# Attention outputs turned by VectorE in 32-squares and divided by their row sums after the gather

## The chip, the core and the metric

The kernel runs on one core of a Trainium2 chip. The core has five engines with queues of their own: TensorE (PE in the profile, with its weight loads as PEld), VectorE (DVE), ScalarE (ACT), GpSimd (POOL) and SyncE (SP), which here only issues DMAs. An instruction starts when those ahead of it in its engine's queue have started and the semaphores that it waits for are set. Sixteen DMA engines move data between DRAM and SBUF, and within SBUF. The metric is the time of one execution on the device, in microseconds (us); of several runs the median is given.

## The reference

The first half is attention with a threshold, for 8 batches, 8 heads, 576 positions and 64 dimensions per head. The second half routes each of the 4608 tokens to one of 8 experts by a hash of its id, and runs a two-layer network.

```python
scores = scale * np.matmul(q, k.transpose(0, 1, 3, 2))
thresh = np.max(scores, axis=-1, keepdims=True) - tau
scores = np.where(scores >= thresh, scores, -1000000000.0)
scores = scores - np.max(scores, axis=-1, keepdims=True)
attn = np.exp(scores)
attn = attn / (np.sum(attn, axis=-1, keepdims=True) + 1e-09)
attn_out = np.matmul(attn, v)
x = attn_out.transpose(0, 2, 1, 3).reshape(B * S, H * D)   # 4608 x 512
expert_idx = token_ids * 2654435761 % E                    # E = 8, F = 1024
for e in range(E):
    xe = x[expert_idx == e]
    out[expert_idx == e] = np.maximum(xe @ w1[e], 0.0) @ w2[e]
```

## The kernel before

**Attention** goes by pairs: two heads of one batch, 32 pairs `p` in all (8 batches for each of 4 head pairs `hp`). A pair has five steps `s`, and one loop counts them through, `n = 5 p + s`. Step 0 takes the last 64 queries of both heads, steps 1 to 4 take 128 queries each. The order of all instructions is written out by hand in that loop (it stands under `manual_schedule`, so no scheduler moves them), and it is a software pipeline. In step `n`:

- `score(n + 1, j)` (L219): PE multiplies queries by keys into one of two PSUM tiles `sc`.
- `negate(n, j)` (L230): VectorE copies the negated scores to `ns` and keeps the row's minimum. GpSimd then makes the threshold `thr` from it (L237). `expo(n, j)` (L244): ScalarE's exponential.
- `mask(n - 1, j)` (L255): VectorE compares with `thr`, multiplies with the exponential into `w`, and sums each row into `rs`.
- `turn_w(n - 2, j)` (L266): PE turns `w`, in 64-wide pieces, through the one PSUM tile `tr`; ScalarE copies the result to `wT` (L282, L287).
- `av_part` (L297): PE multiplies `wT` by the values of pair `q = p - 1` into the PSUM tile `av`, which then holds outputs as 128 dimensions (two heads) by positions. ScalarE copies that to `oT` (`put_oT`, L313), the first 320 columns in step 2, the last 256 in step 4.

So a pair's outputs are complete when the next pair is in its step 4. In step 0 of the pair after that (`s == 0 and p >= 2`), `turn_o` turns them back with ten PE instructions (L266 again, but into `av` from `oT`), and `put_xm` (L336) multiplies them on VectorE by the reciprocals `rec` of the row sums, to which `add_eps` (L327) added 1e-9 on GpSimd and L670 took the reciprocal. Three DMAs on SP's queue then write the normalized rows of the pair to the scratch tensor `x_dram` in DRAM, `x_scratch` in the profile: 512 pieces of 512 bytes (L342) and twice 64 of 256 bytes (L347).

SP's queue also has the loads, in order of the loop: keys and queries of pair `p + 2` and values of `p + 1` in step 0 (L174 to L196), then the x writes, then in some pairs a 2 MB weight tensor in step 2 (pairs 20, 22, 24, 26). GpSimd scales the next pair's keys in step 1 (`scale_k`, L199).

**Routing** runs beside attention. `route()` has small VectorE operations, one or two per step, in pairs 0 to about 16; `scatters()` writes each token's number to its expert's slots with GpSimd DMAs after that.

**The first expert begins early.** From pair 26 on (`n >= G0`), the steps 2, 3 and 4 each issue one `fetch_0` on GpSimd: an indirect DMA (L110) that gathers 128 tokens' rows for one head pair into `xg`, for five blocks of tokens and the first three head pairs, 15 in all. `x_dram` is tracked as a whole: a gather waits for the x writes issued before it, and an x write waits for the gathers issued before it. After the last pair the fourth head pair follows (five gathers). `early_xT` turns `xg` on PE (L555): the first three head pairs at `n == LAST` (160, one past the last step), the fourth after the last gathers. `early_h` (L579) has 48 pieces of the first expert's first product, and `fill(n)` puts `n` of them into PE's queue at places where PE would have nothing to do.

**Experts.** For expert `e`, `turn_x(e + 1)` turns the next expert's gathered rows in 32-squares on VectorE (L856), and 16 DMAs put the squares in place (L861); `gemm1` (L784) and `gemm2` (L802, L815) are PE's products, with evictions on ScalarE and VectorE; the output rows leave by indirect DMAs (L841). `fetch(e + 2)` gathers while expert `e` is in its second product.

## Time and profile before

| | us |
|---|---|
| median of 3 runs | 1004.77 |
| lowest, highest | 1003.88, 1005.04 |
| the profiled execution | 1003.3 |
| its span, first to last instruction | 1001.3 |
| PE busy in the span | 983.8 |
| VectorE busy | 517.7 |
| ScalarE busy | 436.9 |
| GpSimd busy | 291.7 |
| DMA packets | 145779, 117.07 MB |
| of these under 512 bytes | 59860 |

How to read it: the profile comes from one execution, recorded by the hardware. A line of a timeline has the start in us from the beginning of the span, the length in us, the engine, the line of the kernel, the operation, what it writes `<-` what it reads, its shape, and in brackets the idle time before it with what ended it. A group line has the busy time and the mean in ns of one instruction. Lengths of successive instructions of one engine overlap by some hundredths, so the spacing of starts is what one more instruction costs. The end of a matmul is modelled, and a PE that shows as busy need not be at its peak. A wait for several semaphores is put down to the one that came last by the profile; where the engine named had long been done, it was another, often a DMA.

### The profile page before, as it was taken

Reading aid. Unit: us, or ns where it says so; the run is one execution under the profiler, and the core shown is the slowest. Engines: PE = TensorE matmul, PEld = TensorE weight load, DVE = VectorE, ACT = ScalarE, POOL = GpSimd, SP = SyncE. Lnnn points to the kernel's source line nnn. Section 1 sums busy time; section 2 is a strip of 40 time slices with the busy share of each in tenths; the row PEclk is TensorE's granted clock in tenths of the full one; section 3 lists DMA queues with packets and bytes.
Section 4 is the critical chain, followed back from the end, with each engine's and each line's share of the span. In section 5 each row is a group of like instructions: output and inputs, shape, how many; then the busy total and the mean of one; then the engine's idle time right before and its main releaser. Section 6 shows DMA issues by size and latency. Waiting matters only on the chain.

```text
span 1001.3 us, 20487 instructions
## 1 busy us (share of the span) xinstructions
PE 983.8 (98%) x7562; PEld 653.9 (65%) x7562; DVE 517.7 (52%) x1378; ACT 436.9 (44%) x714; POOL 291.7 (29%) x413
## 2 busy tenths in 40 slices
PE   7999999999999999999999999999999999999995
PEld 4666666666666666666766857768578577685773
DVE  7999999999999999994311010010101100200000
ACT  5988888888988889883200000010010000100000
POOL 3233323377676335550321030030210300300101
PEclk9999999999999999999999999999999999999998
DMA  7355544564467677410166344272352533801001
GB/s 182 74 129 141 129 117 112 136 141 107 92 185 169 154 195 194 114 49 25 39 189 185 116 105 143 91 211 89 106 163 84 158 91 104 222 1 39 27 10 57
DMA packets 145779, 117.07 MB, mean 117 GB/s; under 512 B 59860, under 2 KB 120280, under 8 KB 145680
## 3 DMA queue, kind: packets, MB, share of 16 engines
q1 hardware_dynamic: 135408, 96.41, 37.9%
q0 software_dynamic: 7824, 18.91, 6.1%
q8 instruction: 61, 1.00, 0.4%
q10 hardware_dynamic: 2448, 0.44, 0.2%
q14 instruction: 38, 0.31, 0.1%
HBM read 81.99 MB, written 22.37 MB: 104 GB/s over the span
## 4 chain that ended last, share of the span: by engine, by line
PE 87%; issue 6%; SPq 2%; DMA 2%; ACT 1%; DVE 1%; POOL 0%; POOLq 0%; ACTq 0%
PE sc L784 20%; PE av L297 17%; PE sc L219 15%; PE o_ps L802 12%; PE tr L266 10%; PE sc L815 8%; PE sc L579 3%; SPq L835 2%; PE av L266 1%; DMA out_dram<-o_last,gidx 1%; DMA out_dram<-o,gidx 1%; ACT w L244 1%; PE xT_ps L596 0%; PE sc L596 0%; ACT wT_a L287 0%
## 5 line engine op out<-in xcount | busy, mean ns | idle before, releaser
L244 ACT ACTIVATE w<-ns,nmx 128x576 f32<-128x576 f32 x288 | 220.3, 776 | 33.2 <-DVE ns L230 33.1
L784 PE MATMUL sc<-xT,w_sb 128*128 128x304 f32 x896 | 230.4, 419 | 0.0
L255 DVE SCALAR_TENSOR_TENSOR w<-ns,thr,w 128x576 f32<-128x576 f32 x288 | 225.4, 814 | 0.4 <-POOL thr L237 0.4
L784 PEld LDWEIGHTS sc<-xT,w_sb 128*128 128x128 f32 x896 | 170.2, 190 | 61.4 <-issue 3.3
L230 DVE TENSOR_SCALAR_CACHE_REDUCE ns<-sc 128x576 f32<-128x576 f32 x288 | 205.2, 744 | 6.3 <-PE sc L219 5.6
L219 PE MATMUL sc<-k_sb,q 64*128 64x288 f32 (+1 forms) x1280 | 179.2, 426 | 0.6 <-DVE ns L230 0.4
L802 PE MATMUL o_ps<-w_sb,h 128*128 128x512 f32 (+2 forms) x400 | 166.2, 575 | 0.0
L266 PEld LDWEIGHTS tr<-ident,w 64*128 64x128 f32 x2624 | 106.6, 139 | 88.7 <-ACT wT_b L287 26.3
L237 POOL TENSOR_SCALAR thr<-nmx,drop 128x2 f32<-128x2 f32 (+1 forms) x160 | 101.8, 637 | 176.7 <-DVE ns L230 163.4
L792 DVE TENSOR_SCALAR h<-sc 128x608 f32<-128x608 f32 x28 | 22.2, 791 | 240.9 <-PE sc L784 240.9
L266 PE MATMUL tr<-ident,w 64*128 64x64 f32 x2624 | 139.3, 231 | 2.7 <-ACT wT_a L287 2.0
L804 ACT COPY o<-o_ps 128x512 f32<-128x512 f32 (+2 forms) x25 | 14.2, 569 | 274.5 <-PE o_ps L802 248.1
L802 PEld LDWEIGHTS o_ps<-w_sb,h 128*128 128x128 f32 x400 | 74.9, 190 | 86.8 <-issue 84.7
L841 POOL DMA_INDIRECT out_dram<-o,gidx x24 | 23.9, 996 | 324.0 <-ACT o L804 291.4
L219 PEld LDWEIGHTS sc<-k_sb,q 64*128 64x128 f32 (+1 forms) x1280 | 93.0, 179 | 22.9 <-DVE ns L230 9.7
L297 PE MATMUL av<-wT_a,v 128*64 128x320 f32 (+1 forms) x704 | 100.4, 418 | 0.0
L790 ACT ACTIVATE h<-sc 128x608 f32<-128x608 f32 x28 | 19.0, 677 | 182.0 <-PE sc L784 182.0
L815 PE MATMUL sc<-h,w_sb 128*128 128x224 f32 x512 | 98.2, 352 | 0.0
L815 PEld LDWEIGHTS sc<-h,w_sb 128*128 128x128 f32 x512 | 96.9, 190 | 1.1
L287 ACT COPY wT_a<-tr 128x512 f32<-128x512 f32 (+1 forms) x128 | 81.7, 638 | 20.7 <-PE tr L266 20.1
L287 ACT COPY wT_b<-tr 128x512 f32<-128x512 f32 (+1 forms) x128 | 81.2, 634 | 6.4 <-PE tr L266 4.0
L297 PE MATMUL av<-wT_b,v 128*64 128x256 f32 x640 | 83.2, 389 | 0.0
(118 smaller groups left out, 547.9 us busy)
## 6 DMA issues: line engine op xcount, KB each, us to landing
w_sb<-in_moe_w_dram SPq DMA_DIRECT2D x16, 2048.0 KB
q<-in_q_dram SPq DMA_DIRECT2D x62, 288.0 KB
v<-in_v_dram SPq DMA_DIRECT2D x32, 256.0 KB
x_scratch<-xm SPq DMA_DIRECT2D x32, 256.0 KB
xT<-xq SPq DMA_DIRECT2D x84, 80.0 KB
k_sb<-in_k_dram SPq DMA_DIRECT2D x31, 144.0 KB
k_sb<-in_k_dram SPq DMA_DIRECT2D x32, 112.0 KB
o_last<-oq SPq DMA_DIRECT2D x210, 16.0 KB
```

Of the source, the lines that this page charges most:

```text
L219: nc.tensor.matmul(sc[out_rows, i, 0:S2], lhsT=q_sb[rows, h, q0:q1], rhs=k_sb[rows, h], start=True, stop=True)
L230: nc.vector.tensor_scalar(out=ns[:].rearrange("p (i s) -> p i s", i=2), in0=sc[:, :, 0:S2], scalar1=-1.0, scalar2=None, op0=ALU.mult, op1= ...
L237: nc.gpsimd.tensor_scalar(out=thr[:, 0:j + 1], in0=stats[n][0][:, 0:j + 1], scalar1=drop[:], scalar2=None, op0=ALU.add)
L244: nc.scalar.activation(w, nss[n, j][:], AF.Exp, bias=stats[n][0][:, j:j + 1], scale=-1.0)
L255: nc.vector.scalar_tensor_tensor(out=w, in0=nss.pop((n, j))[:], scalar=stats[n][1][:, j:j + 1], in1=w, op0=ALU.is_le, op1=ALU.mult, accum_ ...
L266: nc.tensor.transpose(dst[:, r, 64 * c:64 * c + 64], src[rows, c0:c0 + P], ident[rows, rows])
L287: nc.scalar.copy(dst, tr[:, :, 0:64 * n_c].rearrange("p r (c q) -> p r c q", c=n_c))
L297: nc.tensor.matmul(av[64 * j:64 * j + 64, g, c0:c1], lhsT=v_sb[:, c, 64 * j:64 * j + 64], rhs=wT[g][:, i, c0:c1], start=(c == 0), stop=stop)
L579: nc.tensor.matmul(h_ps[:, i, 0:CH], lhsT=w1_sb[:, co, fo * P:fo * P + P], rhs=xT_0[:, co, i * CH:i * CH + CH], start=(co == 0), stop=(co ...
L784: nc.tensor.matmul(h_ps[:, i, 0:width], lhsT=w1_sb[:, co, fo * P:fo * P + P], rhs=xT[:, co, i * width:i * width + width], start=(co == 0), ...
L802: nc.tensor.matmul(o_ps[:, 0:width], lhsT=h_sb[:, fo, FIRST[kt]:FIRST[kt] + P], rhs=w2_sb[:, fo, cols], start=(fo == 0), stop=(fo == FO - 1))
L815: nc.tensor.matmul(oT_ps[:, i, c * OW:c * OW + OW], lhsT=w2_sb[:, fo, co * P:co * P + P], rhs=h_sb[:, fo, FIRST[KF]:CAP], start=(fo == ord ...
```

## The change

Attention's outputs are no longer turned by PE, nor normalized before they are written. `oT` becomes two tiles, of 320 and 256 columns. `turn_o(p, g)` is now one VectorE transpose in 32 by 32 squares from `oT[g]` into `xo`; the first stands in step 3 between the two `negate`s of the step, the second in step 0 where `put_xm` stood. In `xo` a partition holds one position out of 32 and a run of 32 dimensions, so `put_x` writes pieces of 128 bytes: four DMAs of 576 pieces each. `put_sums`, in step 1, writes the raw row sums to two further columns beside each head pair's 128 (three DMAs of 8- and 4-byte pieces); a row of `x_dram` grows from 512 to 520 numbers, and gathers bring the sums along. The steps take the 64 odd queries first instead of last, so that the 32-squares fit.

The division comes after the gather. For the first expert's first three head pairs GpSimd adds 1e-9 per gathered block (step 1 of pairs 27 to 31), VectorE takes one reciprocal, and GpSimd multiplies: two blocks in step 3 of pair 31 and three in step 4. For the fourth head pair VectorE does all three, between the last gathers and `early_xT`; `fill` is redistributed round it (22 pieces before, 8 after, and the two ahead of the former last `turn_o` are dropped). For the other experts `normalized` does it on VectorE in `turn_x`. At the start the identity is made inside the hand-written order, PE gets 17 instead of 16 turns of it, and the keys' scale is computed in one operation ahead of `drop`.

```diff
+    DX = P + 2
+    x_dram = nc.dram_tensor("x_scratch", (N, HP * DX), FP32, kind="Internal").ap()
...
+    xr_0 = [consts.tile([P, KT, n, 2], FP32, name=f"xr_{n}") for n in (HP - 1, 1)]
...
+    def normalize(engine, dst, xg, rec):
+        engine.tensor_tensor(
+            out=dst.rearrange("p h (j d) -> p h j d", j=2),
+            in0=xg[:, :, 0:P].rearrange("p h (j d) -> p h j d", j=2),
+            in1=rec[:, :, :, None].to_broadcast([P, rec.shape[1], 2, D]), op=ALU.mult)
...
-        def turn_o():
-            turn(av, oT, [(P * (t + 1), P * (t + 1)) for t in range(NQ)] + [(64, 0)])
+        def turn_o(p, g):
+            if g == 0:
+                xo = a_x.tile([P, S // 32, 32], FP32, name="xo")
+                xos[p] = xo
+            c0, c1 = ((0, WA // 32), (WA // 32, S // 32))[g]
+            nc.vector.transpose(out=xos[p][:, c0:c1],
+                                in_=oT[g][:].rearrange("p (c s) -> p c s", s=32))
...
+        def put_x(p):
+            r0, c0 = x_place(p)
+            xo = xos.pop(p)
+            for i in range(4):
+                nc.sync.dma_start(
+                    out=x_dram[r0:r0 + S, c0 + 32 * i:c0 + 32 * i + 32].rearrange(
+                        "(c s) m -> s c m", s=32),
+                    in_=xo[32 * i:32 * i + 32])
+
+        def put_sums(p):
+            r0, c0 = x_place(p)
             rs = rss.pop(p)
-            for i, cols in ((0, 9), (9, 1)):
-                nc.gpsimd.tensor_scalar(out=rec[:, i:i + cols], in0=rs[:, i - i // 9:i - i // 9 + cols],
-                                        scalar1=1e-9, scalar2=None, op0=ALU.add)
...
+                out=x_dram[r0 + 64:r0 + S, c0 + P:c0 + DX].rearrange("(t p) j -> p t j", p=P),
+                in_=rs[:, 0:8].rearrange("p (t j) -> p t j", j=2))
             for j in range(2):
+                nc.sync.dma_start(out=x_dram[r0:r0 + 64, c0 + P + j:c0 + P + j + 1],
+                                  in_=rs[64 * j:64 * j + 64, 8:9])
...
                 if s == 1 and 0 <= q < NP:
-                    add_eps(q)
+                    put_sums(q)
...
-                if s == 2 and 0 <= q < NP:
-                    nc.vector.reciprocal(recs[q][:], recs[q][:])
-                if n == LAST + NS:
-                    fill(2)
-                if s == 0 and p >= 2:
-                    turn_o()
...
+                if s == 3 and 0 <= q < NP:
+                    turn_o(q, 0)
                 if s == 0 and p >= 2 and n != LAST:
-                    put_xm(p - 2)
+                    turn_o(p - 2, 1)
+                    put_x(p - 2)
...
+                k = p - (NP - KT)
+                if s == 1 and 0 <= k < KT:
+                    nc.gpsimd.tensor_scalar(out=xr_0[0][:, k], in0=xg_bufs[k][:, 0:HP - 1, P:DX],
+                                            scalar1=1e-9, scalar2=None, op0=ALU.add)
+                if n == LAST - 3:
+                    nc.vector.reciprocal(xr_0[0][:], xr_0[0][:])
+                for k in {LAST - 2: (0, 1), LAST - 1: (2, 3, 4)}.get(n, ()):
+                    normalize(nc.gpsimd, xg_bufs[k][:, 0:HP - 1, 0:P], xg_bufs[k][:, 0:HP - 1],
+                              xr_0[0][:, k])
...
-            fill(FO * 2 * (CO - 1) - 18)
+            fill(FO * 2 * (CO - 1) - 26)
+            for kt in range(KT):
+                nc.vector.tensor_scalar(out=xr_0[1][:, kt], in0=xg_bufs[kt][:, HP - 1:HP, P:DX],
+                                        scalar1=1e-9, scalar2=None, op0=ALU.add)
+            nc.vector.reciprocal(xr_0[1][:], xr_0[1][:])
+            for kt in range(KT):
+                normalize(nc.vector, xg_bufs[kt][:, HP - 1:HP, 0:P], xg_bufs[kt][:, HP - 1:HP],
+                          xr_0[1][:, kt])
+            fill(8)
...
+        def normalized(k, xg):
+            xr, xn = xr_bufs[k % 2], xn_bufs[k % 2]
+            nc.vector.tensor_scalar(out=xr[:], in0=xg[:, :, P:DX], scalar1=1e-9, scalar2=None,
+                                    op0=ALU.add)
+            nc.vector.reciprocal(xr[:], xr[:])
+            normalize(nc.vector, xn[:], xg, xr)
+            return xn[:].rearrange("p h d -> p (h d)")
...
                 nc.vector.transpose(out=xq[:, :, 32 * k:32 * k + 32],
-                                    in_=xg_sets[e % 2][k][:].rearrange("p (d a) -> p d a", a=32))
+                                    in_=normalized(k, xg_sets[e % 2][k]).rearrange(
+                                        "p (d a) -> p d a", a=32))
```

## The prediction

> **What bounds the kernel now.** I read the page's busy shares and chain first, then stretches of one period, then the timelines of VectorE, GpSimd and SP, and the groups by shape. The page says that TensorE never rests:
>
> ```profile
> PE 983.8 (98%) x7562; PEld 653.9 (65%) x7562; DVE 517.7 (52%) x1378; ACT 436.9 (44%) x714; POOL 291.7 (29%) x413
> ...
> PE 87%; issue 6%; SPq 2%; DMA 2%; ACT 1%; DVE 1%; POOL 0%; POOLq 0%; ACTq 0%
> ```
>
> The slices show two stages: attention to about 470 us with VectorE at 9 tenths, then the experts with VectorE at 1 tenth. The change works in the first. One pair of heads takes 13.90 us there. The stretch below is one such period; its columns after the length are busy us of PE, PEld, DVE, ACT and POOL, then clock, DMA share and GB/s:
>
> ```profile
> 260.00:273.90 13.90, 13.90 (x176) 8.81 (x176) 13.84 (x39) 12.28 (x21) 9.92 (x13) 1.00 0.47 107
> ```
>
> Both PE and DVE look full. Which one sets the pace shows where VectorE gets extra work. Two starts of the same instruction a period apart, and one between them, from VectorE's timeline (start, length):
>
> ```profile
> 119.73 0.81 DVE L336 TENSOR_TENSOR xm<-av,rec 128x640 f32<-128x640 f32 x1
> ...
> 126.94 0.45 DVE L434 TENSOR_TENSOR incl<-incl,onehot 128x288 f32<-128x288 f32 x1
> ...
> 133.65 0.81 DVE L336 TENSOR_TENSOR xm<-av,rec 128x640 f32<-128x640 f32 x1
> ```
>
> With a routing operation worth 0.37 us from start to start the period is 13.92; without it, from L336 at 273.94 to L336 at 287.83, it is 13.89. So VectorE has some 0.35 us to spare in a bare period, and PE sets it. From starts on VectorE: nine L255 at 0.738, nine L230 at 0.678, L336 at 0.736, and the reciprocal, net 0.07 because the next L230 is shorter by as much: 13.55. The gaps that make up the rest stand before L230 (0.11 and 0.06, waiting for scores) and in one L255 (0.13, beside GpSimd's L199).
>
> [...] L255[...] takes 0.87 instead of 0.74 from start to start where L199 runs. [...] L199, with one input, takes 746 ns for 576 elements. [...] In the trace's packet records the 256-byte writes to x_scratch take 17 ns against 26 for 512 bytes, and the 128-byte pieces of o_last<-oq 13: small pieces waste rate[...]. No 128-byte piece goes to DRAM here.
>
> **Part by part: attention.** The groups by shape (busy us, mean ns of one, idle before):
>
> ```profile
> L336 DVE TENSOR_TENSOR xm<-av,rec 128x640 f32<-128x640 f32 x32 | 26.1, 817 | 0.1
> ...
> L266 PE MATMUL av<-ident,oT 64*128 64x64 f32 x320 | 16.8, 232 | 0.2 <-ACT oT L313 0.2
> ...
> L856 DVE STREAM_TRANSPOSE xq<-xg 128x512 f32<-128x512 f32 x15 | 10.3, 704 | 42.6 <-issue 22.9 <-DMA o_last<-oq 14.3 <-DMA xg<-x_scratch,gidx_x 5.4
> ```
>
> PE loses ten turns a pair: from the first (287.01) to the next group (287.37) is 0.36 us, so PE's period becomes 13.54. VectorE loses L336 and L670 (0.81) and gains a 320- and a 256-wide transpose. L856 holds 128x512 at 0.605 start to start within a run (526.63, four in 2.52), which is 0.533 for the elements at 1.04 ns and 0.07 fixed; so 0.405 and 0.339, together 0.74. VectorE's own sum is 13.49, or 13.6 with L199's hindrance. Both engines ran full side by side at 13.92, so I take 13.6 as the new period: 0.3 less in some 12 pairs without routing. In some 14 pairs with routing (13.93 to 14.26) VectorE keeps most of it, about 0.15 each. Bounds: 0.06 a pair (VectorE alone counts) and 0.36. Sum: 12 x 0.3 + 14 x 0.15 = **-5.7** (-2 to -9).
>
> GpSimd's two additions a pair (L327) leave; they are hidden in its idle time. DMA: 640 pieces a pair become 2304 of 128 bytes and 640 of 4 or 8. At 13 and 9 ns that is 2.2 us of 16 engines against 1.0 before, and the DMA share of a period is 0.47: hidden. SP issues 15 DMAs a pair instead of 11, at about 0.6 each 9 us of 13.9: hidden too, except where somebody waits for them:
>
> **The gathers of the first expert.** In pairs 26 to 30 GpSimd fetches three times a pair, and each first fetch waits for all x writes issued so far. GpSimd's threshold (L237) stands behind it, and VectorE's mask (L255) behind that:
>
> ```profile
> 412.78 1.08 POOL L110 DMA_INDIRECT xg<-x_scratch,gidx  x1 [0.17 <-issue]
> ...
> 418.01 0.37 SPq L342 DMA_DIRECT2D x_scratch<-xm  x1
> ...
> 422.80 1.45 POOL L110 DMA_INDIRECT xg<-x_scratch,gidx  x1 [2.94 <-DVE w L255]
> ...
> 424.29 0.30 POOL L237 TENSOR_SCALAR thr<-nmx,drop 128x2 f32<-128x2 f32 x1
> ...
> 424.83 0.81 DVE L255 SCALAR_TENSOR_TENSOR w<-ns,thr,w 128x576 f32<-128x576 f32 x1
> ```
>
> The wait named "DVE w" is for the writes (two L347 follow the one shown, issued by 420.47); the write at 418.01 waits in turn for the gather begun at 412.78. The threshold is ready 0.24 us before it is needed: the slack is spent. After the change seven issues stand in place of three: 0.37 + 6 x 0.62 = 4.1 us instead of 1.5, so the next fetch starts about 6.1 us after the first write instead of 3.6 (408.75 after 405.17). Against that, VectorE reaches its mask some 0.3 later (the transpose stands before it). In pair 27, late already behind a weight load, I expect a stall of 2.0. In 28 and 29 the loop itself sets the pace: 3.8 from first to third fetch, 4.4 till the next write (3.7 without loads beside it, up to 6.3 with), 6.1 to the next fetch: 14.3, and 0.5 for issues as slow as those two L347 (1.02 each). Against 14.06, 13.9 and 13.9 before: 1.5 + 0.9 + 0.9 = **+3.3** (0 to +9).
>
> **GpSimd's normalizing, pair 31.** Five 128x384 operations. [...] (an estimate; low end 0.5, at L199's rate). Two follow the threshold at 449.78 and three the one at 452.90[...]. PE would turn xg at 453.7; the fourth tile is ready at about 456.6, where PE before was done with it at 454.79. PE has no idle time from there to the end to absorb that: **+2.3** (0 to +4).
>
> **The hand-over.** The last ten turns (470.51) go: **-0.4**. The last writes are four issues for three, but nothing has to be turned on PE first; the five fetches begin about where they did (475.72), land by 483.3, and six small additions and a reciprocal, then five 128x128 products, some 1.5 us, end by 485. PE turns the tiles at 487.53 in the trace, about 1.4 earlier with two fill pieces fewer: 1 us of cover, all lost time if the writes land later than that.
>
> **Start and experts.** The first scores may begin 0.8 us earlier, but GpSimd still waits until 11.64 for the second pair's keys with thresholds behind it: 0 (-0.4 to +0.3). In the experts' stage VectorE gains 35 x 1.05 us where it is 85% idle; the turned xT leaves SP at 515.67 and is needed at 531.68: 0.
>
> **Sum.** -5.7 + 3.3 + 2.3 - 0.4 = -0.5: span 1001.3 becomes 1000.8, the profiled run 1003.3 becomes 1002.8, and the median, 1.5 above that run, 1004.77 becomes **1004.3**. A measurement tells 0.2% (2 us) from no change.
>
> **Rivals.** *Everything late is hidden:* the gather loop stays under 13.6 and GpSimd is quick. For: transfers finish early in the other 26 pairs. Against: 0.24 us of slack. 1004.8 - 6.1 = 998.7. *GpSimd's queue becomes the bound (slower):* each loop takes 16.4 (issues of 1 us, as those two L347, and gathers landing 6.3 after their start), 3.7 + 2.5 + 2.5 lost in pairs 27 to 29, and 3.5 at the normalizing: -6.1 + 8.7 - 0.6 (the old periods' own delays) + 3.5 = +5.5, 1010. It decides once a fetch starts more than 5.4 us after the first write (6.1 less the 0.7 by which 14.3 exceeds 13.6). The case that the period doesn't fall at all (VectorE and PE wait for each other) ends there too. *The small pieces are dear in DRAM:* a pair leaves 53% of 16 engines for 13.9 us, 118 us, and the old writes free 15; less 6 for the sums, 2304 pieces fit if each takes under 55 ns. At 65 they cost 1.4 us a pair, +43: 1047[...].
>
> **Chances.** Balanced sum 0.42 (own range 1001 to 1007), all hidden 0.17, GpSimd bound 0.28, small pieces 0.12. Faster: 0.17 and 0.12 of the balanced case; same: 0.19 of it; slower: the rest. The range takes in the first three: 997.5 to 1013.
>
> **What would show it.** A bare period near 13.6 with L336 gone and two transposes of about 0.5 and 0.43 us; VectorE waiting for the threshold in pairs 27 to 29 only; fetches about 6 us after the first x write; PE idle before its first turns of xg; DMA share about 0.1 higher. Wrong I would be if the period stays at 13.9, if 128-byte packets take over 50 ns, or if PE waits at the last tile.

## The result, and the profile after

The changed kernel takes **1099.64 us** (median of 6 runs, 1095.41 to 1104.39); the kernel before takes 1004.1 us (median of 6, 1002.18 to 1005.04). The ratio is 1.0954 (95% interval 1.0924 to 1.0983): slower by 9.5%. The forecast was 1004.3, range 997.5 to 1013.

The page of the kernel after, its busy line, the slices of the DMA share, the queue that SP fills, and the chain that ended last:

```profile
PE 1005.5 (92%) x7243; PEld 656.8 (60%) x7243; DVE 559.5 (51%) x1493; ACT 440.2 (40%) x714; POOL 305.6 (28%) x359
...
DMA  7555679998999699855521653626345272431102
...
q1 hardware_dynamic: 211184, 96.62, 52.6%
...
PE 58%; DMA 13%; issue 11%; ACT 5%; SPq 4%; POOL 3%; DVE 3%; POOLq 0%; DVEq 0%; ACTq 0%
```

TensorE carried 87% of the chain before and carries 58% now; DMA rose from 2% to 13%. The nines of the DMA slices stand in attention, from about 165 us on. Stretches of 50 us show the same; the columns after the length are busy us of PE, PEld, DVE, ACT and POOL, then clock, DMA share and GB/s. The kernel before, and then after:

```profile
200.00:250.00 50.00, 50.00 (x624) 31.13 (x622) 49.88 (x141) 43.15 (x71) 36.20 (x44) 1.00 0.54 122
300.00:350.00 50.00, 50.00 (x636) 31.70 (x636) 49.68 (x139) 44.13 (x73) 25.51 (x38) 1.00 0.69 162
```

```profile
100.00:150.00 50.00, 48.82 (x578) 29.23 (x576) 50.00 (x137) 42.74 (x71) 17.67 (x20) 1.00 0.58 115
200.00:250.00 50.00, 44.14 (x500) 26.56 (x496) 41.58 (x119) 38.79 (x62) 27.28 (x30) 0.97 1.13 115
300.00:350.00 50.00, 43.01 (x486) 26.08 (x486) 40.44 (x112) 36.94 (x60) 25.79 (x30) 1.00 0.99 132
```

From 100 to 150 us the DMA share is 0.58 and VectorE is full. In the two later stretches the 16 engines are full (the share of 1.13 means that records of packets overlap) while they move fewer bytes a second than before, and PE and DVE both idle: neither is the bound. What VectorE and TensorE wait for, from the list of waits (total us, times, longest):

```profile
DVE w L265 <- POOL thr L247: 60.2, 21, 14.9
...
PE tr L276 <- DVE w L265: 45.7, 14, 13.3
...
PE tr L560 <- DVE xg L123: 4.5, 1, 4.5
PE sc L560 <- POOL xg L123: 2.0, 2, 1.1
```

VectorE's wait for the threshold was 0.4 us before. What the change did to the instructions themselves is in the groups by shape; the transposes are as the forecast had them (0.50 and 0.43 us), but two GpSimd rows are not:

```profile
L209 POOL TENSOR_SCALAR k_sb<-k_sb,k_scale 128x576 f32<-128x576 f32 x31 | 62.0, 2000 | 8.8 <-DMA k_sb<-in_k_dram 8.3
...
L331 DVE STREAM_TRANSPOSE xo<-oT 128x320 f32<-128x320 f32 x32 | 16.1, 504 | 14.2 <-DMA x_scratch<-xo 9.2 <-DMA k_sb<-in_k_dram 5.0
L331 DVE STREAM_TRANSPOSE xo<-oT 128x256 f32<-128x256 f32 x32 | 13.9, 435 | 0.0
...
L123 POOL TENSOR_TENSOR xg<-xg,xr 128x384 f32<-128x384 f32 x5 | 6.0, 1220 | 0.0
```

The scaling of the keys, L199 before, took 746 ns; as L209 it takes 2000.

**Where the 95.8 us are.** A pair's period runs from its first mask (L255 before, L265 after) to the next pair's; pairs count from 0. From VectorE's timelines, in us of one profiled run each (spans 1001.3 and 1097.1):

| stretch | before | after | difference |
|---|---|---|---|
| to the first mask | 10.1 | 8.7 | -1.4 |
| pairs 0 to 9 | 141.3 | 145.1 | +3.8 |
| pairs 10 to 25 | 223.4 | 259.8 | +36.4 |
| pairs 26 to 30 (first expert's early fetches) | 69.7 | 113.9 | +44.2 |
| pair 31 to the end | 556.8 | 569.7 | +12.9 |

The packet records tell what happens at pair 10. The 128-byte pieces take 15.6 ns on average in pairs 2 to 9 and 33.1 in pairs 10 to 25, the 8-byte sums 9.1 and 46.6; the medians stay at 13 and 9 to 11, so it is a part of the packets that becomes very long: of the 128-byte ones in pairs 10 to 25, 7.5% take over 100 ns, the longest 1794, and these make up 45.5% of the time of all. Packets of 512 bytes stay as they were (39.4 and 37.2), but the 520-byte zeros that fill the last head pair's columns in pairs 7 to 15, which begin off the multiples of 32 bytes, rise from 37.3 to 154.9. Pair 10 is where the second head pair's outputs are first written. A head pair's block is 130 columns, 520 bytes, and a row 2080: the first head pair's pieces begin on multiples of 32 bytes, the other three's do not.

Long packets and full DMA engines do not by themselves slow the pairs. Pairs 10 to 13 take 56.6 us in all, for 56.1 before, and pairs 23 and 24 take 28.2, for 27.8. The loss of pairs 10 to 25 stands in pairs 14 to 22 (150.5 us for 125.5) and in pair 25 (24.4 for 13.9). The stretches of pairs 10 to 13 and 14 to 22 in the kernel after:

```profile
153.80:210.30 56.50, 55.60 (x652) 33.48 (x652) 56.44 (x163) 49.01 (x81) 22.63 (x25) 1.00 1.11 106
210.30:360.80 150.50, 131.95 (x1488) 79.84 (x1484) 125.10 (x348) 112.99 (x181) 79.89 (x89) 0.98 0.99 116
```

The DMA engines are full in both; VectorE stays full in the first. In the second GpSimd also issues the scatters of the routing (L493), each of which waits for the last but one, into the same table, to land. From the list of waits in pairs 10 to 25 (153.8 to 413.6 us):

```profile
DVE w L265 <- POOL thr L247: 23.1, 15, 3.9
POOL slot_scratch L493 <- DMA slot_scratch<-tok,slot_i: 23.0, 9, 5.5
...
DVE xo L331 <- DMA x_scratch<-xo: 9.2, 1, 9.2
```

In the kernel before, the scatters waited 1.0 us in all for a landing there, and the masks nowhere for a threshold. So the late landings reach VectorE through GpSimd's queue, in which the thresholds stand behind the scatters; in pair 25 they reach it through a buffer of xo that is not free. Pairs 26 to 30, where GpSimd fetches, are the subject of the second group of experiments.

The stalls also go with a slower TensorE. In pairs 26 to 30 its granted clock was 0.82, where the same pairs of the kernel before had 1.00:

```profile
413.60:527.40 113.80, 77.73 (x812) 48.26 (x810) 68.72 (x191) 61.87 (x101) 39.64 (x49) 0.82 0.72 88
```

From 579.3 to 585.9 us it was 0.50, and twelve products of the first expert (L584) took 6.30 us there, for 3.34 in granule_8 below. How much of the last two rows of the table the clock makes was not tried.

### The profile page after: what moved, and what is told of

The parts are those of the page before. It is cut to its first block, busy times and chain, and to the rows that moved or that the text cites. A ratio compares the mean times of both kernels' runs of the same rounds, so it can differ in the third digit from the quotient of the medians.

```text
span 1097.1 us, 20016 instructions
## 1 busy us (share of the span) xinstructions
PE 1005.5 (92%) x7243; PEld 656.8 (60%) x7243; DVE 559.5 (51%) x1493; ACT 440.2 (40%) x714; POOL 305.6 (28%) x359
## 4 chain that ended last, share of the span: by engine, by line
PE 58%; DMA 13%; issue 11%; ACT 5%; SPq 4%; POOL 3%; DVE 3%; POOLq 0%; DVEq 0%; ACTq 0%
PE sc L814 18%; PE o_ps L832 11%; PE sc L845 8%; PE av L307 8%; PE sc L229 7%; DMA x_scratch<-xo 6%; PE tr L276 5%; ACT wT_a L297 3%; DMA k_sb<-in_k_dram 2%; DMA x_scratch<-rs 2%; DVE ns L240 2%; SPq L865 1%; ACT w L254 1%; PE sc L584 1%; SPq L342 1%
## 5 line engine op out<-in xcount | busy, mean ns | idle before, releaser
L265 DVE SCALAR_TENSOR_TENSOR w<-ns,thr,w 128x576 f32<-128x576 f32 x288 | 230.7, 832 | 60.7 <-POOL thr L247 60.2
L254 ACT ACTIVATE w<-ns,nmx 128x576 f32<-128x576 f32 x288 | 222.7, 777 | 49.4 <-DVE ns L240 48.0
L240 DVE TENSOR_SCALAR_CACHE_REDUCE ns<-sc 128x576 f32<-128x576 f32 x288 | 207.9, 746 | 11.7 <-PE sc L229 10.9
L276 PEld LDWEIGHTS tr<-ident,w 64*128 64x128 f32 x2624 | 112.2, 142 | 162.8 <-issue 58.8
L229 PE MATMUL sc<-k_sb,q 64*128 64x288 f32 (+1 forms) x1280 | 191.2, 439 | 14.8 <-DVE ns L240 14.3
L276 PE MATMUL tr<-ident,w 64*128 64x64 f32 x2624 | 144.3, 235 | 57.3 <-DVE w L265 45.7
L247 POOL TENSOR_SCALAR thr<-nmx,drop 128x2 f32<-128x2 f32 (+1 forms) x160 | 88.3, 553 | 194.1 <-DVE ns L240 180.5
L307 PE MATMUL av<-wT_a,v 128*64 128x320 f32 (+1 forms) x704 | 104.6, 431 | 0.0
L307 PE MATMUL av<-wT_b,v 128*64 128x256 f32 x640 | 86.7, 402 | 0.0
```

The lines of the kernel that those rows point to most:

```text
L229: nc.tensor.matmul(sc[out_rows, i, 0:S2], lhsT=q_sb[rows, h, q0:q1], rhs=k_sb[rows, h], start=True, stop=True)
L240: nc.vector.tensor_scalar(out=ns[:].rearrange("p (i s) -> p i s", i=2), in0=sc[:, :, 0:S2], scalar1=-1.0, scalar2=None, op0=ALU.mult, op1= ...
L247: nc.gpsimd.tensor_scalar(out=thr[:, 0:j + 1], in0=stats[n][0][:, 0:j + 1], scalar1=drop[:], scalar2=None, op0=ALU.add)
L254: nc.scalar.activation(w, nss[n, j][:], AF.Exp, bias=stats[n][0][:, j:j + 1], scale=-1.0)
L265: nc.vector.scalar_tensor_tensor(out=w, in0=nss.pop((n, j))[:], scalar=stats[n][1][:, j:j + 1], in1=w, op0=ALU.is_le, op1=ALU.mult, accum_ ...
L276: nc.tensor.transpose(dst[:, r, 64 * c:64 * c + 64], src[rows, c0:c0 + P], ident[rows, rows])
```

## Experiments: where a piece lies

Theory A, from the packets: a 128-byte piece is slow where it begins and ends inside a 32-byte unit (33.1 ns, for 15.6 where it begins on a multiple of 32). A unit here is no more than the 32 bytes between two such multiples, and one that a piece fills in part is called broken; what the hardware does with it no trace shows. Rivals: B, small pieces are slow as such; C, the sums' pieces are the slow ones; D, the longer key scaling on GpSimd holds everything up.

**granule_8.**

```diff
-    DX = P + 2
+    DX = P + 8
...
-                rs_new = a_st.tile([P, 9], FP32, name="rs")
-                rss[p] = rs_new
-            u = 8 if s == 0 else 2 * (s - 1) + j
+                rss[p] = rs_bufs[p % 4]
+            u = 8 * 4 if s == 0 else 8 * (s - 1) + j
...
```

> The changed kernel with a block of 136 columns (544 bytes) for each head pair in place of 130 (520 bytes), so that every piece begins and ends on a multiple of 32 bytes; the sums are written with their six padding zeros, 32 bytes at a time (the last 64 rows' in 4 and 28). The number of packets is the same. If pieces that begin and end inside a 32-byte unit are what DRAM takes slowly (they do from the second head pair on, where the slow packets begin), the 128-byte packets stay near 14 to 17 ns in all pairs, VectorE's period near 14.0 to 14.3, and the time falls to 1008 to 1018. If small pieces are dear as such, it stays above 1080.

**pads_8.** The same DX, put_sums as in the change, and the padding zeroed from xg_bufs[0] beside L665.

> As granule_8 (blocks of 136 columns, so that every 128-byte piece of the attention's output lies on multiples of 32 bytes), but the sums go as the change has them, in pieces of 8 and 4 bytes that fill no 32-byte unit; the padding is zeroed once, in pairs 7 to 15. If the displaced 128-byte pieces are what DRAM takes slowly, this stays within 1% of granule_8: a ratio to before of 1.015 to 1.03. If the short sums are, the slow packets come back and the ratio is above 1.06.

**whole_rows.**

```diff
-            for i in range(4):
-                nc.sync.dma_start(out=x_dram[r0:r0 + S, c0 + 32 * i:c0 + 32 * i + 32]...
+            nc.sync.dma_start(
+                out=x_dram[r0:r0 + TAIL, c0:c0 + P].rearrange("(p t) m -> p t m", p=P),
+                in_=xo[:, 0:16].rearrange("p (t a) s -> p t (a s)", a=4))
+            nc.sync.dma_start(out=x_dram[r0 + TAIL:r0 + S, c0:c0 + P],
+                              in_=xo[0:64, 14:18].rearrange("p a s -> p (a s)"))
```

> The changed kernel with the same bytes of attention's output written as 576 pieces of 512 bytes in two DMAs instead of 2304 of 128 in four. The pieces still begin at odd places (multiples of 520 bytes), and the sums are untouched; the values go to the wrong columns, so the output is not the reference's. A 512-byte piece has two broken 32-byte units, as a 128-byte piece has, so there are a quarter as many. If the broken units of the pieces are the cost, the ratio to before falls from 1.095 to 1.00 to 1.03. If it is the sums (their 640 pieces are all broken units), it stays above 1.06.

**before_pieces**, from the kernel before; its expectation's opening words mean the change of the piece size alone.

```diff
-                out=x_dram[r0:r0 + TAIL, c0:c0 + P].rearrange("(t p) m -> p t m", p=P),
-                in_=xm[:, 0:NQ])
...
+            for i in range(4):
+                c1 = c0 + 32 * i
+                nc.sync.dma_start(
+                    out=x_dram[r0:r0 + TAIL, c1:c1 + 32].rearrange("(t p) m -> p t m", p=P),
+                    in_=xm[:, 0:NQ, 32 * i:32 * i + 32])
...
```

> The kernel before, with its 512 KB-free change alone: each 512-byte and 256-byte write of a row to x_scratch is cut into 128-byte pieces (2304 a pair, eight DMAs for three), all on multiples of 128 bytes; no sums are written. If small pieces are dear as such, it is slower by 40 us or more. If only their place matters, it stays within 3 us of 1004 and the 128-byte packets take 13 to 17 ns throughout.

**granule_4**: granule_8 with DX = P + 4.

> As granule_8, but blocks of 132 columns (528 bytes): pieces of the first and third head pair begin on multiples of 32 bytes, those of the second and fourth on odd multiples of 16. If the unit is 32 bytes, the 128-byte packets are slow (over 25 ns) where the second head pair is written, in pairs 10 to 17, fast (14 to 20 ns) in pairs 18 to 25, and slow again from 26 on. If 16 bytes were enough, they are fast throughout; if a later write to a row that was written before is slow whatever its place, all from pair 10 on are slow.

Measured (ratio to before, with interval; stretches in us of the profiled run; mean ns of the 128-byte packets in pairs 10 to 25):

| kernel | ratio | 0 to 9 | 10 to 25 | 26 to 30 | 31 to end | 128 B |
|---|---|---|---|---|---|---|
| after | 1.0954 (1.0924 to 1.0983) | 145.1 | 259.8 | 113.9 | 569.7 | 33.1 |
| granule_8 | 1.0182 (1.0165 to 1.0199) | 145.9 | 225.6 | 85.0 | 559.8 | 17.2 |
| pads_8 | 1.0171 (1.0147 to 1.0195) | 144.9 | 226.5 | 83.6 | 559.8 | 17.1 |
| whole_rows | 1.0138 (1.0119 to 1.0156) | 146.0 | 227.1 | 79.5 | 560.4 | none |
| before_pieces | 1.0190 (1.0173 to 1.0207) | 140.9 | 228.0 | 85.4 | 557.2 | 13.6 |
| granule_4 | 1050.1 us, one run; before 1008.3 | 146.2 | 228.2 | 101.0 | 563.6 | 22.0 |

Six columns of padding take away some 77 us of the 95: A holds, for displaced pieces that are issued together (more on that below). granule_8's 1026.7 us still lie above the 1008 to 1018 expected; what keeps it there is the second cause. C falls with pads_8, whose sums are as short as the change's and take 10.1 ns. granule_4 shows the multiples of 32 within one run: its 128-byte packets take 14.8 ns in pairs 2 to 9, 26.4 in pairs 10 to 17 (second head pair, odd multiples of 16), 17.7 in pairs 18 to 25 (third, multiples of 32 again) and 22.7 in pairs 26 to 30 (fourth). Its stretches for the second and, mostly, the third head pair, against the same ones of granule_8:

```profile
156.00:241.00 85.00, 82.29 (x968) 49.73 (x966) 83.29 (x238) 72.40 (x119) 40.30 (x45) 1.00 0.97 119
243.00:355.00 112.00, 109.11 (x1304) 67.67 (x1302) 109.89 (x303) 97.33 (x159) 71.45 (x74) 1.00 0.76 136
```

```profile
156.00:241.00 85.00, 83.55 (x984) 50.80 (x982) 84.78 (x242) 73.76 (x121) 45.18 (x47) 1.00 0.66 125
243.00:355.00 112.00, 110.08 (x1312) 67.99 (x1308) 110.49 (x307) 98.37 (x161) 69.40 (x74) 1.00 0.68 134
```

Multiples of 16 bytes were not enough here (26.4 and 22.7 ns), and a row that was written before isn't slow for that (17.7). B keeps a part at most: before_pieces, all on multiples of 128 bytes and at 13.6 ns a packet, is still 1.9% slower, between the two branches of its expectation, 15.7 us of it in pairs 26 to 30. It also has eight issues in place of three, and no run separates the size of the pieces from the number of issues.

**apart.** whole_rows leaves displaced pieces of 512 bytes, which are fast (all packets of that size, loads among them, take 34.7 ns, 34.9 before), and the 8-byte sums in pairs 2 to 9 are broken units too, and fast (9.1 ns). So either the number of broken units counts, or that the two neighbours that share one are under way together.

```diff
-        def put_x(p):
+        def put_x(p, pieces=range(4)):
...
-                    put_x(p - 2)
+                    put_x(p - 2, (0,) if n < LAST else range(4))
+                if s in (1, 2, 3) and p >= 2:
+                    put_x(p - 2, (s,))
```

> The changed kernel with its displaced pieces, but the four writes of a pair, whose pieces share a 32-byte unit with their neighbours, are issued a fifth of a pair apart (2.8 us) instead of one behind the other, from three buffers instead of two. The number of packets and of broken units is the same. If the number of broken units is the cost, the 128-byte packets stay near 30 ns from pair 10 on and the ratio to before above 1.06. If it is that two writes to one unit are under way together, they take about 14 ns and the ratio falls to 1.00 to 1.03.

The displaced 128-byte packets take 16.0 ns in pairs 10 to 25, and 11.9 in pairs 26 to 30; pairs 10 to 25 fall from 259.8 to 228.8 us. The number of packets and of broken units is unchanged, so their number alone is not the cost: it takes displaced pieces that are issued together (33.1 ns one DMA behind the other, 16.0 a fifth of a pair apart). Crowding alone is not the cost either, since crowded and aligned pieces, in granule_8, are fast (17.2 ns). Whether the shared unit of two neighbours makes the cost, or only many broken units at once, is not separated: spreading takes away both. For the second speaks that the 520-byte zeros, which share no unit with pieces of those pairs, were slow beside the crowd (154.9 ns) and take 45.4 here. The ratio missed its range: 1.0685 (1.0664 to 1.0706), because pairs 26 to 30 took 120.1 us. That is the second cause.

## Experiments: who waits for the writes

In pair 26 (the writes issued there are those of pair 24) of the kernel before, the timeline of SP and GpSimd (start, length) shows the writes and the first fetch that waits for them:

```profile
374.22 0.54 SPq L342 DMA_DIRECT2D x_scratch<-xm  x1
374.81 1.16 SPq L347 DMA_DIRECT2D x_scratch<-xm  x2
...
378.93 1.13 POOL L110 DMA_INDIRECT xg<-x_scratch,gidx  x1 [0.94 <-DMA x_scratch<-xm]
```

The same in the kernel after (SP's, GpSimd's and VectorE's timelines):

```profile
425.69 2.22 SPq L342 DMA_DIRECT2D x_scratch<-xo  x4
428.00 0.47 SPq L351 DMA_DIRECT2D x_scratch<-rs  x1
428.51 1.17 SPq L355 DMA_DIRECT2D x_scratch<-rs  x2
...
440.54 1.09 POOL L113 DMA_INDIRECT xg<-x_scratch,gidx  x1 [23.84 <-issue]
441.68 0.31 POOL L247 TENSOR_SCALAR thr<-nmx,drop 128x2 f32<-128x2 f32 x1
...
442.02 0.82 DVE L265 SCALAR_TENSOR_TENSOR w<-ns,thr,w 128x576 f32<-128x576 f32 x1 [14.86 <-POOL thr L247]
```

That write is issued 12.1 us after the pair's first mask. The fetch starts 14.9 us after it, not 4.7, and VectorE's mask waits 14.86 us for the threshold behind it. With aligned pieces, in granule_8, the pieces are quick and the wait is still there:

```profile
388.68 2.76 SPq L342 DMA_DIRECT2D x_scratch<-xo  x4
391.53 0.45 SPq L351 DMA_DIRECT2D x_scratch<-rs  x1
392.02 1.18 SPq L355 DMA_DIRECT2D x_scratch<-rs  x2
...
396.42 1.10 POOL L113 DMA_INDIRECT xg<-x_scratch,gidx  x1 [12.71 <-issue]
...
397.91 0.82 DVE L265 SCALAR_TENSOR_TENSOR w<-ns,thr,w 128x576 f32<-128x576 f32 x1 [9.02 <-POOL thr L248]
```

Here the fetch comes 7.7 us after the first write, but SP issues that write late: pair 26 began at 380.6 by VectorE's mask, and the write is issued 8.1 us after that; in the kernel before it is issued at 374.22, 0.6 us ahead of the first mask. SP's timeline has no pause from the writes issued in pair 25 (377.88) to here; before it had one of 6.3 us (361.85 to 368.20).

SP is not late all along. With all fifteen issues a pair, granule_8 issues the first write ahead of the pair's first mask in pairs 2 to 22 (by 0.1 to 2.1 us), but 4.3 us behind it in pair 23 and 9.8 in pair 24. In between SP's timeline has:

```profile
335.81 6.88 SPq L207 DMA_DIRECT2D v<-in_v_dram  x2
...
347.83 3.84 SPq L504 DMA_DIRECT2D sidx<-slot_scratch  x8
351.72 3.19 SPq L508 DMA_DIRECT2D stok<-slot_scratch  x4
354.96 1.93 SPq L508 DMA_DIRECT2D stok_odd<-slot_scratch  x4
```

The list of SP's waits puts 5.9 us of the first line down to a 2 MB weight load that had not landed, and the other three are the routing's tables. The kernel before has the same loads, but waited 0.7 us for a weight load there and was 1.2 us behind its mask in pair 24. In pair 26 before_pieces, with eight issues for three, is 7.1 us behind, and whole_rows, with five, 3.2.

**fetch_v and granule_fetch_v**, from the change and from granule_8:

```diff
+    v_rows = bass.AP(tensor=v.tensor, offset=0, ap=[[P, N * HP], [1, P]])
...
-        gather(x_rows, xg_bufs[kt][:, hp], gidx_0[:, kt, hp:hp + 1])
+        if hp < HP - 1:
+            gather(v_rows, xg_bufs[kt][:, hp, 0:P], gidx_0[:, kt, hp:hp + 1])
+        else:
+            gather(x_rows, xg_bufs[kt][:, hp], gidx_0[:, kt, hp:hp + 1])
```

> The changed kernel, where the fifteen early fetches of the first expert read rows of the input v instead of x_scratch, so they wait for no write of attention's output (the first expert's input is wrong by that, its work is the same). Pairs 26 to 30 took 120 us after the change where they took 70 before. If GpSimd's fetches that wait for the writes to land, with the thresholds queued behind them, make most of that, these pairs fall to 14 to 17 us each and the ratio to before from 1.095 to about 1.055. If the full DMA engines hold up the loads there, the pairs stay near 24 us and the ratio above 1.085.

> granule_8 with the same edit: the early fetches read the input v. In granule_8 pairs 26 to 30 take 85 us against 70 before. If the waits for the writes are all of that, they take 70 to 72 here and the ratio to before falls from 1.018 to about 1.004. If it stays at 1.018 the loop is not held by the fetches.

(The 120 us that the first of these names are pairs 25 to 29.) fetch_v: 1.0503 (1.0484 to 1.0522); pairs 26 to 30 take 84.4 us for 113.9. granule_fetch_v: 1.0057 (1.0038 to 1.0076); 70.5 us for 85.0, and VectorE's wait for the threshold falls from 17.5 us in all to 2.9. So the ties between fetches and writes (the edit also frees the writes from waiting for fetches) are the loop's whole excess where the pieces are aligned, and two thirds of it where they are not. What is left in fetch_v stands in pairs 26 and 28 (19.8 and 21.1 us), and ahead of the fetches pair 25 takes 24.5, with the DMA share at 0.92 from 384 to 498 us.

**late_fetch.** gate_8 (below) with three buffers for xo, and the fetches a step later:

```diff
-                if n >= G0 and s > 1 and early:
+                if n >= G0 and s > 2 and early:
...
+                if n > G0 and s == 0 and early:
+                    fetch_0(*early.pop(0))
```

> gate_8 with three buffers for the transposed outputs and the early fetches moved, within one DRAM tensor: they stand at the ends of the fourth and fifth step of a pair and at the start of the next, ahead of that pair's writes, instead of at the ends of the third to fifth. The first of them then comes some 11 us after the pair's first write instead of 6. If the waits of pairs 26 to 30 are for writes that have not landed, they go: these pairs take about 14.0 us each, 15 us less in all than in gate_8, and the ratio to before falls from 1.012 to about 0.997, without the double gathers and the longer end of the split. If the writes of seven DMAs need more than 11 us to land, it stays above 1.005.

1.0086 (1.0070 to 1.0102), and 84.4 us in pairs 26 to 30 against 85.0 in gate_8: no gain there, and the expectation's second branch. Pairs 26 and 27 still take 21.8 and 19.8 us; pair 26's writes are issued at 383.21, 9.6 us after its first mask. A later fetch does not help while SP is that late.

## Experiments: where the key scaling falls

Up to pair 9 the DMA engines are not full, yet pairs 5 to 8 take 14.33 us on average where they took 14.00 before. VectorE has no idle time there. Its timeline in pair 8 of the kernel after, with GpSimd's scaling:

```profile
135.49 0.43 DVE L331 STREAM_TRANSPOSE xo<-oT 128x256 f32<-128x256 f32 x1
135.74 0.30 POOL L247 TENSOR_SCALAR thr<-nmx,drop 128x1 f32<-128x1 f32 x1 [1.44 <-DVE ns L240]
135.86 0.77 DVE L265 SCALAR_TENSOR_TENSOR w<-ns,thr,w 128x576 f32<-128x576 f32 x1
136.00 2.23 POOL L209 TENSOR_SCALAR k_sb<-k_sb,k_scale 128x576 f32<-128x576 f32 x1
136.56 1.29 DVE L265 SCALAR_TENSOR_TENSOR w<-ns,thr,w 128x576 f32<-128x576 f32 x1
137.78 0.75 DVE L240 TENSOR_SCALAR_CACHE_REDUCE ns<-sc 128x576 f32<-128x576 f32 x1
```

The second mask takes 1.22 us from start to start instead of 0.74, beside L209. The two instructions lie side by side for 1.29 us, and that cost the mask 0.48 us. Two things changed: the instruction's form (one operation with a scale in SBUF, 2.0 us), and its place. Before, L327 stood ahead of it, which waits for the last masks; without L327 it starts beside a mask instead of behind both.

**scale_two_ops**, from the change, and **before_scale_one**, from the kernel before (the reverse edit):

```diff
-                                    scalar2=None, op0=ALU.mult)
+                                    scalar2=1.0, op0=ALU.mult, op1=ALU.mult)
```

> The changed kernel with one edit: GpSimd's scaling of the keys gets back a second operation (times 1.0), as it had before the change; its one operation took 2000 ns on average after the change where the two took 746 before. If that instruction alone made the change slow (it holds up a mask of VectorE by 0.48 us a pair and GpSimd's thresholds behind it), the time falls from 1099.6 to about 1005. If the writes to DRAM set the pace from pair 11 on, only the pairs before gain, some ten by 0.48 us: 1093 to 1096, with DMA shares near 1 in 200 to 300 us as before.

> The kernel before, with GpSimd's scaling of the keys as the change has it: one multiplication by a scale held in SBUF instead of two operations. If that form is what takes 2.0 us for 0.75 by itself, it takes 2.0 here too, VectorE's mask beside it is held up by about 0.5 us against 0.13, of which VectorE has 0.35 to spare in a period without routing: 0.05 to 0.4 us a pair, so 1006 to 1016. If its length came from the crowded queues after the change, it stays at 0.75 us and the time at 1004.

**gate_one_op**, from granule_8; **gate_8** is the same with the scaling in two operations:

```diff
+                    nc.gpsimd.tensor_scalar(out=rss[q][:], in0=rss[q][:], scalar1=1e-9,
+                                            scalar2=None, op0=ALU.add)
                     put_sums(q)
```

> granule_8, with 1e-9 added to the sums by GpSimd ahead of the key scaling, as the kernel before had it (and one instruction for its two). That addition waits for the last masks, so the scaling, which follows it, no longer starts beside a mask of VectorE but behind it. If the place of the scaling is what costs VectorE 0.48 us a period, the periods of pairs 5 to 8 fall from 14.33 to about 13.9 even with the one-operation form, and the ratio to before falls from 1.018 to about 1.008. If its length of 2 us is what counts, they stay at 14.3.

> gate_one_op with the key scaling in two operations again. If the form matters once the place is right, this is faster than gate_one_op by 0.1 to 0.4 us a pair, 3 to 10 us; else they agree.

scale_two_ops: 1.0719 (1.0679 to 1.0758), and pairs 5 to 8 at 14.33 as without the edit; before_scale_one: 1.0015 (1.0006 to 1.0024), pairs 5 to 8 at 14.00. The form alone moves nothing there. The group in before_scale_one shows that the length belongs to the form, in the old place too:

```profile
L199 POOL TENSOR_SCALAR k_sb<-k_sb,k_scale 128x576 f32<-128x576 f32 x31 | 53.8, 1735 | 6.3 <-DMA k_sb<-in_k_dram 3.5
```

gate_one_op: pairs 5 to 8 at 13.93, ratio 1.0151 (1.0134 to 1.0168), a smaller gain than expected; gate_8: 13.93 again, 1.0120 (1.0103 to 1.0137). Place is what counts in these pairs, 0.4 us each; the form adds 0.3% in all (2.8 us, just under the 3 to 10 expected). D falls as the main cause. scale_two_ops was a miss: it gained 23 us where I had expected 4 to 7. Of the 19.3 us between the profiled runs 12.8 stand in pairs 14 to 22, where the thresholds stand behind the scatters in GpSimd's queue; VectorE's waits for a threshold fell there with it (in pairs 10 to 25 from 23.1 us to 8.8). That fits a queue on the path, in which a shorter instruction counts, but no run took it apart.

## Experiments: all causes taken away

**split_gate.** gate_8 with a second DRAM tensor for the last head pair:

```diff
-    x_dram = nc.dram_tensor("x_scratch", (N, HP * DX), FP32, kind="Internal").ap()
+    x_dram = nc.dram_tensor("x_scratch", (N, (HP - 1) * DX), FP32, kind="Internal").ap()
+    x_last = nc.dram_tensor("x_last", (N, DX), FP32, kind="Internal").ap()
...
```

> gate_8 with the last head pair's columns in a DRAM tensor of their own, so that the early fetches, which read only the other three, wait for no recent write; the experts' gathers become two for each tile. With all three causes gone, pairs 26 to 30 take about 14 us each, bare periods 13.6, and the ratio to before is about 0.995 (0.990 to 1.000): what the forecast called all hidden. If something else of the change costs, it stays above 1.003.

1.0011 (1.0002 to 1.0021): the loop is down to 74.1 us, but pair 28 took 17.7, with VectorE's transpose waiting for a buffer of xo.

**split_gate_3** has three such buffers (`bufs=3` for a_x); **split_gate_3n** also moves early_xT of the first four tiles behind turn_o, put_x and av_part of step LAST; **late_fetch_n** is late_fetch with that move.

> split_gate with three buffers for the transposed outputs instead of two. In split_gate the transpose of pair 28 waited 2.79 us for the writes of the pair before last, and that pair took 17.7 us for 14. If nothing else comes up there, it takes about 14.0 and the ratio to before falls from 1.001 to about 0.998.

> split_gate_3 with TensorE's turns of the first four fetched tiles put behind the next pair's turns and products, where they no longer wait for GpSimd's normalizing (1.13 and 0.90 us idle in split_gate). If TensorE is the bound there, 2 us less than split_gate_3: a ratio of about 0.996. If the first layer's copies come too late instead, no gain.

> late_fetch with TensorE's turns of the first four fetched tiles put behind the next pair's turns and products, as in split_gate_3n, whose gain was 0.0015 of the time: a ratio of about 0.995, faster than before.

split_gate_3: 1.0011 (1.0004 to 1.0018), with pairs 26 to 30 at 69.2 us; split_gate_3n: 0.9996 (0.9988 to 1.0005); late_fetch_n: 1.0095 (1.0076 to 1.0114), no better than late_fetch. All four, split_gate among them, lie above what was expected. In split_gate_3 the saving is there at last: its first mask is at 10.1 us as before, and pair 31's at 440.1, where before it was at 444.5. One bare period of it, pair 22:

```profile
315.60:329.40 13.80, 13.60 (x172) 8.61 (x170) 13.70 (x41) 12.39 (x21) 5.46 (x9) 1.00 0.80 198
```

Nearly all of the 4.4 us is spent again after that: 561.0 us from pair 31's first mask to the end, against 556.8. Of that, 2.9 are GpSimd's last drain, which takes 5.06 us in the three split kernels and 2.20 in before, after, granule_8 and gate_8; it is a cost of the split, not of the change. No version was clearly faster than before.

## Why the prediction was wrong

The measured 1099.64 us lie above every case that was priced, the dearest rival (1047) among them. In ratios to before, the padding takes the excess from 0.0954 to 0.0182 (granule_8), and fetches that wait for no write take it from there to 0.0057 (granule_fetch_v).

**"128-byte pieces at 13 ns ... hidden": the step that failed most.** Aligned, the packets took 13 to 17 ns, so the price was right for them. Displaced and crowded they averaged 33.1, the 8-byte sums 46.6, and the displaced zeros rose with them. "Hidden" failed with the price: the 16 engines were full (DMA share 1.11 and 0.99 in pairs 10 to 13 and 14 to 22), and what waited for landings (scatters, buffers of xo, fetches) held up the masks: +36.4 us in pairs 10 to 25, for +2.2 in granule_8, and +44.2 in pairs 26 to 30, for +15.3. I took 13 ns from SBUF copies and did not look at the addresses, though 520 and 2080 stand in the diff. The rival "small pieces are dear in DRAM" had the place and, at 65 ns, a price that neither the pieces nor the sums reached on average in pairs 10 to 25; its threshold of 55 ns assumed that only the pieces themselves grow, so the sign "over 50 ns" never came. With whole_rows fast at 512 displaced bytes (34.7 ns) and before_pieces at 128 aligned ones (13.6), neither size nor place decides alone.

**"+3.3 for the gather loop": right mechanism, mis-sized.** The chain (writes, fetch, threshold, mask) is the one the traces show, but it costs +15.3 in granule_8 and +44.2 in the change. I priced the seven issues from the first write on, with 0.24 us of slack gone, and took SP's other work as hidden. By its sum it was, up to pair 22; but fifteen issues at 0.6 us fill 9 of 13.9 us only if none of them waits, and the reserve that was left did not carry the wait for the weights and the sixteen table loads. In pair 26 the first write was issued 8.1 us after the first mask instead of 0.6 before it. In granule_8 two of the four writes issued in pair 25 took 3.47 us (377.88). The rival "GpSimd's queue becomes the bound" had this direction, with 8.7 us.

**"GpSimd's two additions leave; hidden": wrong.** They held the key scaling behind the masks; and I never asked what the new form of that scaling costs. Together, and by their place more than their form, they made the periods of pairs 5 to 8 14.33 instead of 13.93.

**"13.6 as the new period, -5.7": right in direction, the period's part too large.** With the other causes gone the bare period is 13.76 to 13.84 (pairs 17 to 23 of split_gate_3), 0.1 less than before and not 0.3, and the gain to pair 31 is 4.4 us. That the total comes this near is luck in part: 2.8 of it stands in pairs 0 to 15, most of them with routing, for which the forecast gave 0.15 each. VectorE's own sum, 13.49 in the forecast, is 13.54 with the transposes as measured, and the period was 13.76 in pair 22: 0.18 of the difference is one gap ahead of an L249 (L240 in the change), and PE is busy 13.60 of 13.80, so the two still take turns at waiting. The transposes cost 0.43 and 0.36 from start to start (forecast 0.405 and 0.339). The 1.04 ns an element and 0.07 us fixed of that forecast fit two instructions of the kernel before: 0.736 us from start to start for 640 elements (L336) and 0.37 for 288 (L434).

**"Normalizing, +2.3; hand-over, -0.4".** The +2.3 rested on 1.0 us for each of the five products, an estimate of mine that no trace had shown. They took 1.22 on average: the one with hardly a mask of VectorE beside it 0.82, the four beside masks 1.30 to 1.34. TensorE waited 2.0 us for them, and from the last mask to TensorE's first product of the last tile granule_8 needs 37.2 us against 34.5 before (+2.7 for +1.9). In the change itself the last tile was late by 4.5 us: the 1 us of cover was gone, as its first fetch began 9.95 us after the first of its last writes was issued, for 4.54 in granule_8.

**Start and experts, 0**: the first mask came 1.4 us earlier, within what that stretch varies by between these runs (8.7 to 10.1); the experts' added VectorE work cost nothing that shows (first to last store of rows is 475.5 us before and after).

## What to carry to other kernels

Before writing rows in pieces, work out the byte address of each piece: 128-byte pieces off the multiples of 32 bytes, issued together with their neighbours, took 33.1 ns here for 17.2 on them, and filled all 16 engines; six columns of padding took some 77 us of the 95 away. Full DMA engines cost 0.5 us in pairs 10 to 13 (share 1.11) and 25.0 in pairs 14 to 22 (0.99); ask which queue waits for a landing, and what stands behind it there. SP's queue, hidden by the sum of its issues (9 of 13.9 us), was not hidden once issues waited and its reserve was gone (8.1 us behind the mask in pair 26 of granule_8); count from when the queue can start, not from the first issue. And an instruction that is removed "from idle time" may have been holding the next one in place: L327's going set the key scaling beside a mask, 0.4 us a pair in pairs 5 to 8.

## What the runs showed of the hardware

- A 128-byte write to DRAM took 13.6 ns on average when aligned to 128 bytes (before_pieces, and granule_8 in pairs 2 to 9), 17.2 aligned to 32 (granule_8 in pairs 10 to 25), 33.1 displaced and beside its neighbours (after), and 16.0 displaced but issued a fifth of a pair apart from them (apart). Medians stayed at 13 in pairs 10 to 25: the cost is in few, long packets (7.5% over 100 ns in after).
- Displaced writes of 512 bytes (34.7 ns against 34.9, loads of that size among them) and of 8 bytes away from the crowd (9.1 ns in pairs 2 to 9 of the change, 10.1 in pads_8) showed no penalty; displaced writes of 8 and 520 bytes beside the crowd did (46.6 and 154.9).
- GpSimd's multiplication of 128x576 by one scalar from SBUF took 1735 ns, and with a second, immediate operand 746, in the same place of the kernel before.
- VectorE's mask lost 0.48 us beside that multiplication, whether GpSimd's took 2.2 us or 1.2 (scale_two_ops).
- GpSimd's product of 128x384 with a broadcast operand took 0.82 us, and 1.30 to 1.34 beside VectorE's masks.
